# Loads 6 and 7 of a DeltaNet and Fourier-mix kernel: the written order on all engines, and the weight conversion moved within load 6

## The chip, the cores and the metric

The kernel runs on one core of one Trainium2 chip. The metric is the device time of one execution in microseconds (us); the median of three runs of the kernel before is 765.58 us (765.42 to 767.2). The core has a matrix engine (PE, with its weight loads listed as PEld), a vector engine (DVE), an activation engine (ACT), a general engine (POOL) and a queue that issues DMA transfers (SP). Each engine works off a queue of its own.

## The reference

Two stages follow each other. The first is a DeltaNet attention over 4 batches, 8 heads, 768 time steps and a head size of 48; the state is a 48 x 48 matrix per head that each step reads and corrects. The second mixes each batch's 768 x 384 result by the real part of a two-dimensional Fourier transform, normalises each row, and adds a two-layer network of width 1536.

```python
for t in range(S):
    y[:, :, t] = np.einsum('bhd,bhde->bhe', q[:, :, t], state)
    v_old = np.einsum('bhde,bhd->bhe', state, kt)
    state = state + bt[:, :, :, None] * np.einsum('bhd,bhe->bhde', kt, vt - v_old)
...
u = x + np.real(np.fft.fft(np.fft.fft(x, axis=1), axis=2))
un = (u - mu) / np.sqrt(var + 1e-06)
return u + np.maximum(un @ w_ch1, 0.0) @ w_ch2
```

The two weights `w_ch1` (384 x 1536) and `w_ch2` (1536 x 384) arrive as 64-bit floats, and the kernel makes 32-bit floats of them itself from the two halves of each word.

## The kernel before

**Loads and periods.** The time steps are cut into loads of 128, six to a batch, so there are 24 loads, numbered 0 to 23, and load 6 is the first of the second batch. `period(g, side)` (line 1000) writes out the work of one load `g` in six slots (the loop over `i`, line 1049). A slot first takes a step of each generator in `pieces[i]`, then steps of the inversion and of the conversion, then the generators in `behind[i]`, and last some steps of `side`, the network of the batch before.

**The generators.** Each of them issues a few instructions and yields.

- `step(g, c)` (line 678) carries the state over half a load. In the second batch it forms the products `pair<-S,KT`, subtracts them on DVE (`V`, line 698), forms `one<-V,MT`, copies that on ACT (`U`, line 708), forms `pair<-U,K` and adds it to the state on DVE (`S`, line 739, or a copy at line 737 for the first half of a batch).
- `pre_q(g)` (line 531) turns the queries: four PE products, a copy on ACT (line 320), then PE products and a masked product on DVE (`LQ`, line 555).
- `outputs(g)` (line 742) makes the attention's result: PE, a copy on ACT (line 762), PE, an addition on DVE (line 772), and for the first load of a batch one more copy on ACT (line 774).
- `invert16(r)` (line 458) inverts the small triangular matrices of round `r`, four loads to a round. It yields 46 times: a transpose on DVE (line 475, 32 x 32 blocks), a square root on ACT (line 481), eleven short DVE instructions (lines 483 to 504), three at lines 506 to 510, 30 instructions that each need the one before (lines 517 and 520 in turn), and two transposes on DVE (lines 523 and 525). Round 2 is needed by load 8.
- `pre_m16(g)` (line 598) uses that inverse. For load 8 it begins in slot 2 of period 7 with two copies on ACT (`Z`, line 608), and then the PE products `one<-Z,GU`.
- `weight(last)` (line 224) converts one weight in twelve pieces of 128 x 384. A piece `i` is worked in two halves. The first half has an ACT instruction (line 276) and a DVE instruction (line 277) for piece `i` and two ACT instructions (lines 281, 282) for piece `i - 1`. The second half has DVE instructions: line 289 for piece `i - 2`, and lines 293, 297 and 299 for piece `i`. Line 299 frees the staging buffer, and SP then issues the load of piece `i + 3` (line 257). In loads 6 and 7 it is `w_ch2` that is converted; the name `conv` holds this generator.
- `fourier(b)` (line 818) ends in one pass for each 128 rows: PE products, a copy on ACT (`Q`, line 873), four DVE additions (lines 882 to 885), two DVE statistics (lines 889, 890) and two small POOL instructions (lines 893, 894).
- `mlp(b)` (line 898), which is `side`, normalises 256 rows (`un`, two DVE instructions, line 909), turns them (six PE transposes `ptr` and two ACT copies `unT`, line 920), forms the first layer in twelve pieces (`ph`, six matmuls each, with an ACT copy at line 930), and then the second (`po`, line 937, with a DVE addition at line 941).

**The end of the first batch.** Lines 1281 to 1291 write out, one after the other, twelve pieces of `ph`, the conversion's pieces 0 to 7, the last four passes of `fourier(0)`, and at the end `un` for the second group of rows (line 1291). The last pass of `fourier` comes before the conversion's piece 7, and both before this `un`.

**What sets the order.** Inside a `tc.manual_schedule(engines=...)` block, the instructions of the engines that are named stand in their queues in the order in which the code issues them. For other engines the framework's planner orders the queue by its own estimate of when each instruction can go. In the kernel before, the code up to line 1292 and from line 1298 on names PE, DVE, ACT and POOL. Lines 1294 to 1297, which hold the end of `pre_q(6)` and the periods 6 and 7, name PE alone. SP is named nowhere.

In period 6 a slot advances the inversion by 5 and the conversion by 2 (by 4 in the last slot). In period 7 it advances the inversion by 8 in each of slots 0 and 1, which ends it.

Of the kernel before, what the change touches and what calls it, by code (L numbers as in the profile page):

```python
# [64 lines left out]
def kernel(  # L65
# [14 lines left out]
    NL = S // L  # L80
# [56 lines left out]
    def halves(dst, src, g, engine):  # L137
        b, n = divmod(g, NL)
        for c in range(2):
            for hh in range(2):  # L140
                t0 = n * L + c * C
                (engine or nc.sync).dma_start(
                    out=dst[hh * C:hh * C + C, c],
                    in_=src[b, 4 * hh:4 * hh + 4, t0:t0 + C, :].rearrange("j t d -> t j d"))
# [16 lines left out]
    def load_k(g, engine=None):  # L161
        if g < NLT:
            halves(Ks[g % 3].rearrange("p (c j) d -> p c j d", c=2)[:, :, :, 0:D], k, g, engine)

    def load_v(g, engine=None):
        if g < NLT:
            Vs[g] = wk.tile([128, 2, 4, D], F32, tag="V", bufs=2, name="V")
            halves(Vs[g], v, g, engine)
# [3 lines left out]
    def load_beta(r, engine=None):  # L172

        if r * RL >= NLT:
            return
        t = wk.tile([128, W], F32, tag="beta", bufs=2, name="beta")
        i = 0
        while i < RL:
            b, n = divmod(RL * r + i, NL)
            m = min(RL - i, NL - n)  # L180
            for q4 in range(4):
                hh, blk = divmod(q4, 2)
                p0 = q4 * W + i * 8
                src = beta[b, 4 * hh:4 * hh + 4, n * L:(n + m) * L].rearrange(
                    "j (c b t) -> b c j t", b=2, t=W)[blk]
                (engine or nc.sync).dma_start(out=t[p0:p0 + 8 * m], in_=src)
            i += m
        betas[r] = t
# [553 lines left out]
    def outputs(g):  # L742

        b, n = divmod(g, NL)
        pre.pop(g)
        (QT, LQ), U0 = LQs.pop(g), Us.pop(g)
        if n == 0:
            xs[b] = wk.tile([128, NL, DM], F32, tag="x", bufs=2, name="x")
        x = xs[b][:, n, :]
        pq = ps_pair()  # L750
        for j in range(2):
            for hh in range(2):
                for cc in range(2):
                    for jp in range(2):
                        if n == 0 and cc == 0:
                            continue
                        o = (2 * hh + j) * D
                        mm(pq[full[cc], jp, o:o + D], QT[lo[jp], hh, j, cc * C:cc * C + C],
                           S[(b, 2 * n + cc)][lo[jp], hh, j, :], j == 0 and hh == 0)

        rw = full[1] if n == 0 else slice(0, 128)
        nc.scalar.activation(x[rw].rearrange("p (i a e) -> p a i e", a=2, e=D),
                             pq[rw, :, 0:4 * D].rearrange("p a (i e) -> p a i e", e=D), ACT.Copy)
        yield
        pl = ps_pair()
        for j in range(4):
            for cc in range(2):
                for hh in range(2):
                    mm(pl[full[cc], hh, D * j:D * j + D], LQ[full[hh], cc, j, :],
                       U0[full[hh], cc, j, :], j == 0)  # L770
        xv = x.rearrange("p (h e) -> p h e", h=2)
        nc.vector.tensor_tensor(xv[rw], xv[rw], pl[rw, :, 0:4 * D], op=ALU.add)
        if n == 0:
            nc.scalar.activation(xv[full[0]], pl[full[0], :, 0:4 * D], ACT.Copy)
        yield
# [182 lines left out]
    def advance(gen, n=1):  # L958
        for _ in range(n):
            if next(gen, "end") == "end":  # L960
                return False
        return True

    def drain(gen):
        for _ in gen:
            pass
# [33 lines left out]
    def period(g, side):  # L1000


        nonlocal pm, inv, late, done, fold
        b, n = divmod(g, NL)
        r, li = divmod(g, RL)
        more = g + 1 < NLT
        last_round = (r + 1) * RL >= NLT
        load_k(g + 2)
        c0, c1 = step(g, 0), step(g, 1)
        if n > 0:  # L1010
            pieces = [[c0], [c0], [c0], [c1], [c1], [c1]]
        else:
            pieces = [[], [c0], [c0], [c1], [c1], [c1]]
        behind = [[] for _ in range(SLOTS)]
        if late:

            for i in (1, 2) if n == 1 and b == 1 else (0,):
                pieces[i].append(late)
        if n + 1 < NL:
            late = outputs(g)  # L1020
            if g > NL:
                pieces[4].append(late)
        else:

            pieces[5] = []
        fresh = more and li == RL - 1
        if more:
            nq = pre_q(g + 1)
            behind[0].append(nq)
            pieces[2].append(nq)  # L1030
            if g + 1 >= RL * R16:
                pm = pre_m(g + 1)
                pieces[3 if fresh else 1].append(pm)
                pieces[5 if fresh else 3].append(pm)
            elif g + 1 >= 2 * RL:
                pm = pre_m16(g + 1)
                if not fresh:
                    behind[0].append(pm)
                for i in range(4):
                    pieces[i + (2 if fresh else 1)].append(pm)  # L1040
        if not last_round and r > 1:
            if li == 0:
                load_beta(r + 1)
            keys = {0: ((0, 1), (2, 3), (4, 5)), 1: ((0, 1),)}.get(li, ())
            for i, (s0, s1) in enumerate(keys):
                k4 = pre_a(RL * (r + 1) + 3 * li + i)
                behind[s0].append(k4)
                pieces[s1].append(k4)
        for i in range(SLOTS):
            if i == (2 if r + 1 < R16 else 3) and fresh and inv:  # L1050
                drain(inv)
                inv = None
            for p in pieces[i]:
                advance(p)
            if i == 5 and n + 1 == NL:
                o = outputs(g)
                drain(o)
                late = None
            if li == 1 and i == 1 and r > 1 and not last_round:
                inv = invert(r + 1)  # L1060
            if g == NL:
                advance(inv, 5)
                advance(conv, 2 if i < 5 else 4)
            elif inv:
                advance(inv, 8 if r + 1 < R16 else 6)
            if n + 2 >= NL and 0 < i < 5:

                if n + 2 == NL and i == 1:
                    fold = folds(b)
                advance(fold, 2)  # L1070
            at = SLOTS * n + i + 1
            if b > 1:
                want = 2 + (PIECES - KEEP - 2) * at // (SLOTS * NL)
            else:

                want = 2 + KF + (2 + 2 * KF) * at // (2 * SLOTS)
                if n > 1:
                    want = 4 + 3 * KF + (PIECES - KEEP - 4 - 3 * KF) * (at - 2 * SLOTS) // (
                        SLOTS * (NL - 2))
            for p in behind[i]:  # L1080
                advance(p)
            advance(side, want - done)
            done = max(want, done)
        load_v(g + 2)

    engines = {mybir.EngineType.PE, mybir.EngineType.DVE, mybir.EngineType.Activation,
               mybir.EngineType.Pool}
    with tc.manual_schedule(engines=engines):
# [32 lines left out]
        conv = weight(0)  # L1121
# [116 lines left out]
        g = NL - 1  # L1238
# [28 lines left out]
        side, done = mlp(0), 0  # L1267
# [8 lines left out]
        conv = w2s  # L1276
# [14 lines left out]
        advance(side)  # L1291
        done = 3 + KF
        inv = invert16(2)
    with tc.manual_schedule(engines={mybir.EngineType.PE}):
        drain(nq)
        for g in range(NL, NL + 2):
            period(g, side)
    with tc.manual_schedule(engines=engines):
        for b in range(1, B):
            for g in range(max(NL * b, NL + 2), NL * (b + 1)):  # L1300
                period(g, side)

            advance(side, KEEP - 12)
            drain(fold)
            f, then = fourier(b), mlp(b)
            done = 0
            for i in range(4 + NC):
                advance(f)
                advance(side, 12 * (i + 1) // (4 + NC) - done)
                done = 12 * (i + 1) // (4 + NC)  # L1310
                if i in (6, 8):
                    advance(then)
            drain(side)
            side, done = then, 2
        drain(side)
# [30 lines left out]
```

## Time and profile before

| what | value |
|---|---|
| median of three runs | 765.58 us (765.42 to 767.2) |
| the profiled execution, its own time | 767.2 us |
| its span in the profile | 765.3 us |
| mean granted PE clock | 0.955 |
| PE busy | 705.3 us, 92% |
| DVE busy | 378.1 us, 49% |
| ACT busy | 264.3 us, 35% |
| POOL busy | 71.2 us, 9% |

The span runs from the first to the last instruction of the profile; the 1.9 us between the span and the execution's own time lie outside it. All times in the text are counted from the start of the span. The page gives an engine's busy time over the whole span, the views by window give it for a stretch, and the view of waits names for each idle stretch of an engine the instruction that ended it. Busy time of PE can overlap between matmuls, since their ends are modelled.

Periods 6 and 7 lie between about 182 us and 237 us. The stretch from 182 to 192 us has PE busy for 4.18 of 10 us, and DVE for all 10.

### The profile page before, as it was taken

Reading aid. Unit: us, or ns where it says so; the run is one execution under the profiler, and the core shown is the slowest. Engines: PE = TensorE matmul, PEld = TensorE weight load, DVE = VectorE, ACT = ScalarE, POOL = GpSimd, SP = SyncE. Lnnn points to the kernel's source line nnn. Section 1 sums busy time; section 2 is a strip of 40 time slices with the busy share of each in tenths; the row PEclk is TensorE's granted clock in tenths of the full one; section 3 lists DMA queues with packets and bytes.
Section 4 is the critical chain, followed back from the end, with each engine's and each line's share of the span. In section 5 each row is a group of like instructions: output and inputs, shape, how many; then the busy total and the mean of one; then the engine's idle time right before and its main releaser. Section 6 shows DMA issues by size and latency. Waiting matters only on the chain.

```text
span 765.3 us, 23096 instructions
## 1 busy us (share of the span) xinstructions
PE 705.3 (92%) x10198; PEld 542.2 (71%) x10198; DVE 378.1 (49%) x957; ACT 264.3 (35%) x644; POOL 71.2 (9%) x114
## 2 busy tenths in 40 slices
PE   7876788996999987899999999999999999999998
PEld 5676677775866766687867767868677678777684
DVE  5868667479842299625188426369511230700000
ACT  5545554288423422214422333223223222221120
POOL 7000000001000011002110211001100110100000
PEclk8699678998899999999999999999999999999999
DMA  9843332134102321001312221001120000000000
GB/s 152 213 71 80 93 80 54 45 84 134 44 18 65 69 45 39 16 11 32 64 40 44 38 49 39 1 10 43 34 51 16 12 12 1 21 1 21 11 11 21
DMA packets 111862, 36.09 MB, mean 47 GB/s; under 512 B 101873, under 2 KB 109842, under 8 KB 111762
## 3 DMA queue, kind: packets, MB, share of 16 engines
q1 hardware_dynamic: 109938, 33.86, 20.4%
q8 instruction: 80, 1.31, 0.7%
q0 software_dynamic: 640, 0.43, 0.4%
q10 hardware_dynamic: 1184, 0.33, 0.3%
q14 instruction: 20, 0.16, 0.1%
HBM read 29.88 MB, written 4.72 MB: 45 GB/s over the span
## 4 chain that ended last, share of the span: by engine, by line
PE 76%; DVE 15%; ACT 6%; issue 2%; DMA 1%; SPq 0%; ACTq 0%; DVEq 0%
PE po L110 24%; PE ph L110 21%; PE one L110 15%; PE pair L110 10%; PE one L113 2%; PE unread L1101 2%; DVE M L450 1%; DVE tmp L446 1%; PE ptr L113 1%; DVE w L289 1%; DMA C<-in_k_dram 1%; DVE M L520 1%; ACT G L385 1%; DVE tmp L517 1%; PE pf L110 1%
## 5 line engine op out<-in xcount | busy, mean ns | idle before, releaser
L110 PE MATMUL ph<-unT,w 128*128 128x256 f32 x864 | 205.8, 389 | 0.6 <-ACT unT L920 0.6
L110 PE MATMUL po<-w,hT 128*128 128x384 f32 x576 | 205.0, 495 | 0.1
L110 PEld LDWEIGHTS ph<-unT,w 128*128 128x128 f32 x864 | 161.1, 192 | 24.6 <-ACT unT L920 0.9
L110 PEld LDWEIGHTS po<-w,hT 128*128 128x128 f32 x576 | 103.5, 190 | 56.8 <-issue 0.5
L930 ACT ACTIVATE hT<-ph 128x256 f32<-128x256 f32 x144 | 55.3, 384 | 144.8 <-PE ph L110 144.6
L941 DVE TENSOR_TENSOR x<-x,po 128x384 f32<-128x384 f32 x24 | 13.2, 551 | 107.0 <-PE po L110 107.0
L739 DVE TENSOR_TENSOR S<-S,pair 128x192 f32<-128x192 f32 x40 | 14.0, 351 | 76.4 <-PE pair L110 76.3
L110 PEld LDWEIGHTS one<-V,MT 64*64 64x64 f32 x768 | 32.4, 147 | 20.0 <-issue 8.3
L110 PE MATMUL one<-V,MT 64*64 64x48 f32 x768 | 37.7, 234 | 4.2 <-DVE V L698 2.7
L882 DVE TENSOR_TENSOR x<-x,one 128x193 f32<-128x193 f32 x24 | 8.5, 353 | 63.2 <-ACT Q L873 63.2
L450 DVE TENSOR_TENSOR M<-M,tmp 128x31 f32<-128x31 f32 (+15 forms) x93 | 34.7, 373 | 3.2
L446 DVE TENSOR_TENSOR tmp<-A,M 128x31 f32<-128x31 f32 (+15 forms) x93 | 34.1, 367 | 2.5
L110 PE MATMUL one<-MT,ND 64*64 64x64 f32 x768 | 30.6, 234 | 3.5 <-ACT MT L647 3.0
L110 PEld LDWEIGHTS one<-MT,ND 64*64 64x64 f32 x768 | 28.1, 149 | 5.1 <-ACT MT L647 3.4
L698 DVE TENSOR_TENSOR V<-V,pair 128x192 f32<-128x192 f32 x33 | 11.5, 349 | 38.8 <-PE pair L110 30.6
L110 PEld LDWEIGHTS one<-dtab,F 97*128 97x128 f32 (+1 forms) x192 | 25.2, 191 | 5.2 <-ACT F L877 0.5
L110 PEld LDWEIGHTS pair<-U,K 64*64 64x64 f32 x704 | 15.8, 139 | 16.6 <-issue 12.7
L320 ACT ACTIVATE QT<-one 128x512 f32<-128x512 f32 x24 | 14.2, 593 | 38.1 <-PE one L113 38.1
L893 POOL TENSOR_SCALAR rstd<-mv 128x2 f32<-128x2 f32 x12 | 3.9, 325 | 249.4 <-DVE mv L890 249.4
L110 PEld LDWEIGHTS pair<-S,KT 48*64 48x64 f32 x528 | 10.7, 133 | 21.7 <-issue 10.6
L110 PE MATMUL one<-dtab,F 97*128 97x97 f32 (+1 forms) x192 | 25.9, 275 | 0.0
L110 PE MATMUL pair<-KT 48*32 48x64 f32 (+1 forms) x1152 | 21.1, 239 | 4.2 <-ACT KT L320 2.9
(178 smaller groups left out, 1023.8 us busy)
## 6 DMA issues: line engine op xcount, KB each, us to landing
w<-in_moe_w_ch_dram SPq DMA_DIRECT2D x12, 384.0 KB
E<-in_moe_w_ch_dram SPq DMA_DIRECT2D x12, 384.0 KB
out_dram<-x SPq DMA_DIRECT2D x24, 192.0 KB
K<-in_k_dram SPq DMA_DIRECT2D x92, 48.0 KB
V<-in_v_dram SPq DMA_DIRECT2D x92, 48.0 KB
C<-in_k_dram SPq DMA_DIRECT2D x18, 192.0 KB
Q<-in_q_dram SPq DMA_DIRECT2D x18, 192.0 KB
w<-in_q_dram SPq DMA_DIRECT2D x6, 192.0 KB
```

Of the source, the lines that this page charges most:

```text
L110: nc.tensor.matmul(o, lhsT=lhsT, rhs=rhs, start=start, stop=stop, skip_group_check=True)
L113: nc.tensor.matmul(o, lhsT=src, rhs=ident[0:src.shape[0], 0:src.shape[0]], is_transpose=True, start=start, stop=True, skip_group_check=True)
L289: nc.vector.tensor_tensor(dst, man0.rearrange("p (c f) -> p c f", c=c), num0.bitcast(F32).rearrange("p (c f) -> p c f", c=c), op=ALU.mult)
L320: nc.scalar.activation(dst.rearrange("p h j t -> p (h j t)"), pt, ACT.Copy)
L446: nc.vector.tensor_tensor(t, A[:, j + 1:W, j:j + 1].broadcast_to([128, n, j + 1]), M[:, j:j + 1, 0:j + 1].broadcast_to([128, n, j + 1]), o ...
L450: nc.vector.tensor_tensor(M[:, j + 1:W, 0:j + 1], M[:, j + 1:W, 0:j + 1], t, op=ALU.add)
L698: nc.vector.tensor_tensor(R4, R4, pw[:, :, 0:2 * D].rearrange("p a (j e) -> p a j e", e=D), op=ALU.subtract)
L739: nc.vector.tensor_tensor(s1v, s0.rearrange("p h j e -> p h (j e)"), pk, op=ALU.add)
L882: nc.vector.tensor_tensor(near, near, pb[:, 0, 0:MH + 1], op=ALU.add)
L930: nc.scalar.activation(hT[:, fc, :], ph, ACT.Relu)
L941: nc.vector.tensor_tensor(x[:, T, :], x[:, T, :], po, op=ALU.add)
L1101: nc.tensor.matmul(unread[:, 0:DM], lhsT=src[:, 0:128], rhs=src, start=True, stop=True, skip_group_check=True)
```

## The change

The change has two parts. The periods 6 and 7, and the end of `pre_q(6)`, move into the block that names PE, DVE, ACT and POOL. In period 6, the slot's five steps of the inversion are split: three stay where they were, and two come at the slot's end, after the conversion's steps, which move there too, behind `behind[i]` and `side`.

```diff
             if g == NL:
-                advance(inv, 5)
-                advance(conv, 2 if i < 5 else 4)
+                advance(inv, 3)
             elif inv:
                 advance(inv, 8 if r + 1 < R16 else 6)
...
             advance(side, want - done)
             done = max(want, done)
+            if g == NL:
+                advance(conv, 2 if i < 5 else 4)
+                advance(inv, 2)
         load_v(g + 2)
...
         inv = invert16(2)
-    with tc.manual_schedule(engines={mybir.EngineType.PE}):
         drain(nq)
-        for g in range(NL, NL + 2):
-            period(g, side)
-    with tc.manual_schedule(engines=engines):
         for b in range(1, B):
-            for g in range(max(NL * b, NL + 2), NL * (b + 1)):
+            for g in range(NL * b, NL * (b + 1)):
                 period(g, side)
```

`NL` is 6. No instruction is added or taken out; PE's order is the same as before, since PE is named in both.

## The prediction

> **What bounds the kernel now.** I read the page first: PE is busy 92% of the span, and in the windows from 195 to 262 us nearly always, so a delay there moves the end by as much. The exception near the change is the window 182 to 192 us. There I asked for PE's waits (the numbers are us in total, times, longest):
>
> ```profile
> PE ptr L113 <- DVE un L909: 5.8, 1, 5.8
> ...
> PE one L110 <- DVE V L698: 0.9, 1, 0.9
> ```
>
> These two are the stalls that the change can touch: 5.8 us before the transposes of `un`, and 0.9 us in period 7. The timeline shows the first one (start, duration, engine, line):
>
> ```profile
> 181.91 1.99 DVE L475 STREAM_TRANSPOSE A<-G 128x1024 f32<-128x1024 f32 x1 [0.33 <-ACT G L385]
> ...
> 182.94 0.35 ACT L873 ACTIVATE Q<-one 128x193 f32<-128x193 f32 x1
> ...
> 183.82 0.32 DVE L882 TENSOR_TENSOR x<-x,one 128x193 f32<-128x193 f32 x1
> ...
> 184.36 0.29 ACT L481 ACTIVATE nrm<-A 128x32 f32<-128x32 f32 x1
> ...
> 188.68 0.86 DVE L909 TENSOR_SCALAR un<-x,mv,rstd 128x384 f32<-128x384 f32 x2
> ...
> 189.30 1.51 PE L113 MATMUL ptr<-pack,un 128*128 128x128 f32 x6 [5.82 <-DVE un L909]
> ```
>
> The planner has put the inversion's transpose (L475), written after `un`, ahead of the last Fourier pass (L882), while DVE had nothing else to do. It also put L481 ahead of ACT's other work. The written order takes both back. PE's clock falls with the idle stretch (columns: length, PE, PEld, DVE, ACT, POOL busy, granted clock, DMA):
>
> ```profile
> 120.74:124.15 3.41, 1.26 (x72) 1.01 (x68) 2.30 (x7) 2.17 (x4) 0.00 (x0) 1.00 0.25 48
> 182.18:185.59 3.41, 1.30 (x37) 0.98 (x36) 3.41 (x7) 3.41 (x11) 0.00 (x0) 1.00 0.61 167
> 185.59:189.01 3.42, 0.00 (x0) 0.00 (x0) 3.42 (x11) 1.38 (x4) 2.19 (x2) 0.50 0.03 6
> 189.01:192.42 3.41, 3.12 (x24) 2.64 (x25) 3.41 (x14) 2.54 (x6) 0.18 (x1) 0.50 0.37 115
> 192.42:195.83 3.41, 3.41 (x10) 2.69 (x9) 2.89 (x10) 2.31 (x6) 0.00 (x0) 0.50 0.33 115
> ```
>
> The granted clock changes only on the edges of such 3.41 us windows. [...] So `ph` x12 took 4.85 us here against 2.86 us later.
>
> **Part 1, the opening of period 6.** In the written order DVE, free at 181.58, waits for ACT's `Q` copy (182.94 + 0.35 = 183.29). Then come the pass's additions (start to start 0.26 each) and statistics, done at 185.2; conversion piece 7 (0.25 + 0.47 + 0.5 + 0.55 + 0.26, about 2.0 us); `un` starts at 187.2 and the transposes of `un` at 187.7. That is 1.6 us earlier than 189.30, since L475, L555 and another piece's L289 no longer stand in between.
>
> The gain does not get through. `un` is followed on DVE by L555 of load 6 (0.6 us) and then by L475 (2.0 us), to 190.6. On ACT the written order is L481, the copy of the turned queries (L320, 0.59 us), the two copies `unT` (L920, 0.49 us each). L481 needs L475, so all of them queue behind it: 190.6 + 0.28 + 0.5 + 0.4 + 0.5 gives `unT` at 192.2. PE has `one<-V,MT` in between (to 190.6 at half clock) and then waits 1.6 us. `ph` starts at 192.2 against 191.77. **Term: +0.4 us**, of which 0.3 is left at `pair<-U,K` (the clock returns at 195.83 in both).
>
> **Part 2, the slots of period 6.** A slot has two `ph` pieces, 2.78 us. The conversion's ACT step (L276) now queues behind the slot's two `ph` copies, and DVE's L293 behind L276. The second `ph` of slot 1 ends at about 196.9; its copy and L276 take to 197.8; L293, L297, L299 and two inversion steps take to 199.5. Then slot 2 stands on DVE in sequence: L737, L555, three inversion steps (1.6 us), the conversion (2.2 us), L506 to L517 (0.9 us): L698 starts at about 204.0 and ends at 204.4. PE is done with slot 3's `ph` at 203.7 and waits for it 0.7 us. In the trace of before L698 ran at 201.65, ahead of that work, and hid behind `ph`. From slot 4 on there is slack: L739 ends at 209.5 and period 7's first product comes at 212.35 (211.21 before). **Terms 1 and 2 together: +1.1 us.**
>
> **Part 3, period 7.** The timeline of before:
>
> ```profile
> 211.21 0.45 PE L110 MATMUL pair<-S,KT 48*64 48x48 f32 x16
> ...
> 213.59 1.92 DVE L525 STREAM_TRANSPOSE A<-M 128x1024 f32<-128x1024 f32 x1
> ...
> 215.35 0.34 DVE L698 TENSOR_TENSOR V<-V,pair 128x192 f32<-128x192 f32 x1
> ...
> 220.65 0.56 DVE L772 TENSOR_TENSOR x<-x,pair 64x384 f32<-64x384 f32 x1 [0.16 <-PE pair L110]
> 221.06 1.11 PE L110 MATMUL one<-Z,GU 64*64 64x64 f32 x32
> 221.24 0.48 ACT L774 ACTIVATE x<-pair 64x384 f32<-64x384 f32 x1 [3.22 <-DVE x L772]
> ```
>
> From the first product to `one<-Z,GU` PE takes 9.85 us, 0.92 of it the wait for L698 behind L525. The written order puts L698 ahead, which gives the 0.92 us back: 8.9 us. But there the copies `Z` (L608) stand on ACT behind L774, which needs L772, which stands on DVE behind L698, the last 14 inversion steps, both transposes and L739. In sum, from the first product's start: 0.5 (product) + 0.3 + 4.0 (14 steps at about 0.25 and 0.04 between dependent ones) + 2.0 + 1.85 + 0.3 + 0.55 + 0.5 (L774) + 0.9 (two L608) = 10.9 us. PE waits 0.65 us for L739 and 1.1 us for `Z`. **Term: 10.9 - 9.85 = +1.0 us.** After it the order is the same, with DVE idle enough.
>
> **What else moves.** The twelve pieces' DVE and ACT work is the same in number. The last two loads of staged weights follow L299: 187.3 and 194.1 instead of 188.8 and 191.8; a piece landed some 3.6 us after its issue (181.64, ACT released at 185.24) and piece 11 is read at about 203.6, so 5 us cover it. If that cover were gone, DVE would wait for it. SP's next loads wait for PE anyway (197.04). On POOL the zeroing of `M` (L474, 1.0 us, at 75.7 before) moves to period 6 and the scaling of V (L629, 0.83 us) to the end of period 7; POOL is idle there. A DVE step took 0.77 us beside L629 where its neighbours took 0.24, so each may cost DVE 0.5 us or nothing; nothing is my value, since the rows L893 and L894 (1.2 us) beside DVE work stretched themselves and not DVE. A gain there is excluded, as nobody waited for them.
>
> **The sum.** 1.1 + 1.0 = +2.1 to 2.2 us against the profiled execution's own 767.2 us: 769.4 us. The median is 1.6 us lower. I take that as one half-clock window less (3.41 us at half speed is 1.7 us): with the window edges 0.3 us later, 189.01:192.42 would have been full. In the written order the wait of 1.6 us before `ph` keeps that window from being full, so I measure from 767.2. Against the median this is +3.8 us. If the two waits of part 3 (1.75 us) fall into one window, PE is busy 1.66 us of it, at the edge of half, and another window at half clock adds 1.7 us: 771.1.
>
> [...]
>
> **Rivals.**
> - The clock falls in period 7 too: 771.1, and up to 772.7 with 0.5 us each from POOL's two moves and 0.6 us more in the slots.
> - No change: 765.6. DVE's work is the same in sum and is spread; if the slots lose nothing (L698 early enough by 0.7 us), and period 7's chain comes out 1 us shorter, the opening's 0.4 us is left and the clock returns a window early. For it speaks that each margin is under 1.2 us.
> - Faster: `un` comes 1.6 us earlier and `unT` follows it directly. Place: ACT's queue at 188 to 192 us; it decides if L475 is done before the transposes of `un` end (about 189.2). Then `ph` starts at 190.6, 1.1 us early, part 3 gives 0.9 us, and the clock is as in the median: 765.6 - 2.0 = 763.6, or 762 with a further window saved. Against it: L475 comes after `un` and L555 in the code.
> - The change does nothing, if the planner's order was the written one: 765.6. The timeline excludes this (L475 before L882).
>
> **How the numbers follow.** Forecast 769.4: 0.40; clock falls again, 771 to 772.7: 0.30; no change: 0.17; faster: 0.13. About 0.3% (2.3 us) is what a measurement can tell from no change, so "same" is 763.3 to 767.9. The first two cases are slower: 0.70; same 0.17; faster 0.13. The range leaves out the faster case and the far end above: 765.3 to 772.7.
>
> **What would show it.** Part 1: the transposes of `un` near 187.7, ACT's L920 directly after L320 and L481, PE waiting for `unT`. Part 2: PE's second `one<-V,MT` waiting for L698. Part 3: `one<-Z,GU` waiting for L608, and L608 after L774. I am wrong if L920 runs before L481, or if L698 of slot 3 ends before slot 3's `ph`.

## The result and the profile after

The changed kernel takes 770.35 us (median of 4 runs, 769.85 to 770.54) against 765.5 us before: a ratio of 1.0059, 95% interval 1.0042 to 1.0077. It is slower by 0.6%, as forecast, and the time lies within the range, 0.95 us above the predicted 769.4. The profiled execution has a span of 768.6 us, 3.3 us more than before.

PE's order is the same in both kernels, so the n-th matmul of one trace can be set against the n-th of the other. Up to the changed stage the after profile runs 2.7 us ahead, with 51.2 us at half clock before 180 us where the other has 54.6. This has nothing to do with the change, which only begins there. To leave it out I compare a **stretch**: from the start of `pair<-QT,KT` of load 6 to the start of `one<-Z,ND` in period 7. Before:

```profile
182.20 0.69 PE L110 MATMUL pair<-QT,KT 48*64 48x64 f32 x32
...
228.66 1.11 PE L110 MATMUL one<-Z,ND 64*64 64x64 f32 x32
```

After:

```profile
179.54 0.69 PE L110 MATMUL pair<-QT,KT 48*64 48x64 f32 x32
...
229.79 1.11 PE L110 MATMUL one<-Z,ND 64*64 64x64 f32 x32
```

That is 46.46 us before and 50.25 us after: the stretch grew by 3.8 us. The span's 3.3 us are these 3.8, less the 2.7 ahead of the stretch, and 2.2 more behind it (most of them while 10.2 us at half clock stand between 240 and 330 us, where before it was 3.4). Of the 4.85 us between the medians the stretch of these two profiles holds 3.8; where the rest lies is not shown.

Where the stretch grew, the waits of PE show (window 175 to 260 us, those inside the stretch; us in total, times, longest):

```profile
PE ptr L113 <- DVE un L909: 4.8, 1, 4.8
PE ph L110 <- ACT unT L920: 1.7, 1, 1.7
PE one L110 <- ACT Z L608: 1.3, 1, 1.3
PE one L110 <- DVE V L698: 0.7, 1, 0.7
PE pair L110 <- DVE S L739: 0.6, 1, 0.6
```

Two waits of before became five. The first is shorter (4.8 for 5.8), the 0.9 us for V L698 in period 7 is gone, and four new ones, 4.3 us in sum, took their place. In sum PE waits 2.4 us longer (9.1 for 6.7). The timeline of the opening after the change:

```profile
180.27 0.35 ACT L873 ACTIVATE Q<-one 128x193 f32<-128x193 f32 x1
...
180.65 0.36 DVE L882 TENSOR_TENSOR x<-x,one 128x193 f32<-128x193 f32 x1 [1.73 <-ACT Q L873]
...
184.31 0.73 DVE L299 TENSOR_SCALAR O<-E 128x384 int32<-128x384 int32 x1
184.96 0.85 DVE L909 TENSOR_SCALAR un<-x,mv,rstd 128x384 f32<-128x384 f32 x2
...
186.33 1.91 DVE L475 STREAM_TRANSPOSE A<-G 128x1024 f32<-128x1024 f32 x1
...
188.28 0.26 ACT L481 ACTIVATE nrm<-A 128x32 f32<-128x32 f32 x1 [5.80 <-DVE A L475]
...
188.92 0.86 ACT L920 ACTIVATE unT<-ptr 128x384 f32<-128x384 f32 x2
...
189.84 4.51 PE L110 MATMUL ph<-unT,w 128*128 128x256 f32 x12 [1.73 <-ACT unT L920]
```

DVE now stands idle for 1.73 us where the planner had put L475. ACT stands idle for 5.80 us in front of L481, with the copies `unT` behind it. In period 7, first the copies `Z` of the kernel before, then the kernel after:

```profile
213.74 0.91 ACT L608 ACTIVATE Z<-G,pack 128x256 f32<-128x256 f32 x2 [2.04 <-DVE G L523]
```

```profile
210.26 0.35 DVE L698 TENSOR_TENSOR V<-V,pair 128x192 f32<-128x192 f32 x1 [1.33 <-PE pair L110]
...
216.51 1.92 DVE L525 STREAM_TRANSPOSE A<-M 128x1024 f32<-128x1024 f32 x1
...
218.64 0.56 DVE L772 TENSOR_TENSOR x<-x,pair 64x384 f32<-64x384 f32 x1
...
219.62 0.90 ACT L608 ACTIVATE Z<-G,pack 128x256 f32<-128x256 f32 x2
...
220.66 1.98 PE L110 MATMUL one<-Z,GU 64*64 64x64 f32 x32 [1.30 <-ACT Z L608]
```

L698 is ahead of the transposes now, and `Z`, copied at 213.74 before (2.5 us after the period's first product), comes 9.9 us after that product (209.74). The clock, by windows (length, PE, PEld, DVE, ACT, POOL busy, granted clock, DMA):

```profile
217.12:220.53 3.41, 1.62 (x81) 1.35 (x80) 2.74 (x4) 1.28 (x3) 0.00 (x0) 1.00 0.16 29
220.53:223.95 3.42, 3.29 (x34) 2.65 (x35) 0.00 (x0) 1.28 (x3) 0.00 (x0) 0.50 0.02 5
```

The two waits of period 7 left PE busy for 1.62 us of a window, and the next window ran at half clock: `one<-Z,GU` took 1.98 us instead of 1.11. The longer waits (2.4 us) and this window (1.4 us, by the run with unread products in period 7 below) make up the 3.8 us.

### The profile page after: what moved, and what is told of

The parts are those of the page before. It is cut to its first block, busy times and chain, and to the rows that moved or that the text cites. A ratio compares the mean times of both kernels' runs of the same rounds, so it can differ in the third digit from the quotient of the medians.

```text
span 768.6 us, 23101 instructions
## 1 busy us (share of the span) xinstructions
PE 708.8 (92%) x10198; PEld 544.6 (71%) x10198; DVE 380.9 (50%) x957; ACT 263.8 (34%) x644; POOL 69.5 (9%) x114
## 4 chain that ended last, share of the span: by engine, by line
PE 74%; DVE 15%; ACT 7%; issue 2%; DMA 1%; SPq 0%; ACTq 0%; DVEq 0%
PE po L110 23%; PE ph L110 22%; PE one L110 15%; PE pair L110 9%; PE one L113 2%; PE unread L1103 2%; DVE M L450 1%; DVE tmp L446 1%; PE ptr L113 1%; DMA C<-in_k_dram 1%; ACT GU L395 1%; ACT G L385 1%; PE pf L110 1%; DVE LQ L555 1%; DVE w L289 1%
## 5 line engine op out<-in xcount | busy, mean ns | idle before, releaser
L110 PE MATMUL ph<-unT,w 128*128 128x256 f32 x864 | 207.9, 392 | 2.4 <-ACT unT L920 2.4
L739 DVE TENSOR_TENSOR S<-S,pair 128x192 f32<-128x192 f32 x40 | 14.0, 351 | 71.2 <-PE pair L110 71.2
L698 DVE TENSOR_TENSOR V<-V,pair 128x192 f32<-128x192 f32 x33 | 11.5, 350 | 42.0 <-PE pair L110 38.6
L110 PEld LDWEIGHTS pair<-S,KT 48*64 48x64 f32 x528 | 10.7, 133 | 20.1 <-issue 10.9
```

What stands on the lines that cost most here:

```text
L110: nc.tensor.matmul(o, lhsT=lhsT, rhs=rhs, start=start, stop=stop, skip_group_check=True)
L698: nc.vector.tensor_tensor(R4, R4, pw[:, :, 0:2 * D].rearrange("p a (j e) -> p a j e", e=D), op=ALU.subtract)
L739: nc.vector.tensor_tensor(s1v, s0.rearrange("p h j e -> p h (j e)"), pk, op=ALU.add)
```

## The experiments

The times are medians; beside each experiment the kernel before was run on that experiment's chip (765.89 to 765.95 us; the two first rows are from the first comparison). The last column is the stretch in the profile, in which differences outside of the changed stage don't show.

| kernel | us | ratio, 95% interval | stretch, us |
|---|---|---|---|
| before | 765.5 | | 46.46 |
| after | 770.35 | 1.0059 (1.0042 to 1.0077) | 50.25 |
| written order alone | 769.82 | 1.0057 (1.0044 to 1.0070) | 50.55 |
| slots' split alone | 765.78 | 0.9997 (0.9986 to 1.0008) | 46.40 |
| after, L475 and L481 ahead | 766.02 | 1.0000 (0.9990 to 1.0011) | 45.86 |
| after, Z ahead of L774 | 766.44 | 1.0004 (0.9994 to 1.0015) | 47.23 |
| after, 2 unread products in period 7 | 768.62 | 1.0036 (1.0023 to 1.0049) | 48.84 |
| after, 6 unread products in the opening | 768.57 | 1.0037 (1.0024 to 1.0051) | 50.27 |
| after, conversion behind L698 | 769.88 | 1.0054 (1.0037 to 1.0072) | 50.31 |
| after, L475, L481 and Z ahead | 765.48 | 0.9993 (0.9983 to 1.0002) | 44.37 |
| the same, 6 unread products | 763.70 | 0.9962 (0.9947 to 0.9976) | 43.05 |
| before, 6 unread products in the opening | 762.67 | 0.9958 (0.9945 to 0.9971) | 42.92 |

**The two parts of the change, each alone.** First the written order with the slots as before (against the changed kernel):

```diff
             if g == NL:
-                advance(inv, 3)
+                advance(inv, 5)
+                advance(conv, 2 if i < 5 else 4)
...
-            if g == NL:
-                advance(conv, 2 if i < 5 else 4)
-                advance(inv, 2)
```

> Periods 6 and 7 in the written order on all engines, but with the slots as before (five inversion steps and the conversion ahead of the queries' turn and the network). My theory (the loss comes from the written order: unT behind the inversion's square root on ACT, Z behind L774 and L772): unT comes later still, since the conversion's ACT steps also stand ahead of it; laid out by rows the Fourier-mix network's first ph of period 6 starts 1.6 us later than in the changed kernel and one<-Z,GU 1.8 us later, so 771 to 773 us. Rival (the loss comes from moving the conversion to the slot's end): as before, 764.5 to 767 us.

It took 769.82 us, below the expected 771 to 773. The queue did what was expected: the first `ph` starts 11.87 us after the stretch's start instead of 10.30 (1.6 us later), `one<-Z,GU` 42.92 instead of 41.12 (1.8 us later). What was missing is the half clock of period 7: the same waits of 0.6 and 1.3 us lay over two windows, with PE busy for 82% and 62%, and the clock did not fall. PE did not wait for L698 in slot 3. The rival, 764.5 to 767, is out.

The second part alone is the kernel before with the slot's lines of the change, and the planner still ordering DVE, ACT and POOL (the lines of the diff without those that move the periods).

> The inversion's split and the conversion at the slot's end, with the planner still ordering DVE, ACT and POOL in periods 6 and 7. My theory: the planner fills DVE and ACT again and L475 stands ahead of L882, so near the kernel before, 764 to 767 us. Rival (the move of the conversion costs by itself): 769 to 771 us.

765.78 us, ratio 0.9997: no difference. Its timeline shows that the planner undid the written place again:

```profile
181.32 1.98 DVE L475 STREAM_TRANSPOSE A<-G 128x1024 f32<-128x1024 f32 x1 [0.33 <-ACT G L385]
...
183.20 0.34 DVE L882 TENSOR_TENSOR x<-x,one 128x193 f32<-128x193 f32 x1
```

So the loss belongs to the written order, and the split's own share is small: it brings `unT` 1.6 us earlier than the order alone.

**The opening.** In the changed kernel the inversion begins earlier:

```diff
         for fc in range(KF):
...
+            if fc == 10:
+                inv = invert16(2)
+                advance(inv)
             if fc % 3 == 1:
                 advance(f)
...
+        advance(inv)
         advance(side)
         done = 3 + KF
-        inv = invert16(2)
...
             if g == NL:
-                advance(inv, 3)
+                advance(inv, 3 if i else 1)
```

> The changed kernel, with the inversion's transpose L475 written ahead of the last Fourier pass and its square root L481 ahead of un. My theory: L475 falls into DVE's wait for Q, un keeps its time within 0.5 us, unT no longer waits, ph starts 1.6 us earlier, V L698 of slot 3 2.5 us earlier so that PE no longer waits for it; one<-Z,GU 2.5 us earlier, and perhaps one half-clock window less (1.7 us): 766 to 768 us. Rival (the opening is no matter, the slots and period 7 carry the loss): 769.5 to 770.5 us.

766.02 us. The transpose fell into DVE's wait, and `unT` follows the transposes of `un` at once:

```profile
180.24 1.99 DVE L475 STREAM_TRANSPOSE A<-G 128x1024 f32<-128x1024 f32 x1 [0.33 <-ACT G L385]
...
186.65 1.42 PE L113 MATMUL ptr<-pack,un 128*128 128x128 f32 x6 [4.85 <-DVE un L909]
187.47 1.13 ACT L920 ACTIVATE unT<-ptr 128x384 f32<-128x384 f32 x2 [3.37 <-PE ptr L113]
188.00 1.09 PE L110 MATMUL one<-V,MT 64*64 64x48 f32 x16
189.03 3.41 PE L110 MATMUL ph<-unT,w 128*128 128x256 f32 x12
```

`ph` starts 8.51 us after the stretch's start (10.30 in the changed kernel): 1.8 us earlier, 1.6 expected. The half clock lasted one window here instead of three. One point was wrong: PE still waited 0.73 us for L698 in slot 3, as PE had come earlier by as much as DVE. One edit of order takes back the whole loss, against the rival. Part of that came by the clock of period 7. The two waits there (0.6 and 1.3 us) are still in the profile, but they lie over two windows, with PE busy for 81% and 63%, and the clock held. By the run with unread products in period 7 below, this is about 1.4 of the 4.4 us by which the stretch is shorter than in the changed kernel.

**Period 7.** The copies `Z` are written at the end of slot 1:

```diff
-        if g != 2 * RL:
-            yield
+        yield
...
                 advance(inv, 8 if r + 1 < R16 else 6)
+                if g == NL + 1 and i == 1:
+                    advance(pm)
```

> The changed kernel, with the two copies Z (L608) of load 8 written at the end of period 7's slot 1, ahead of L774 on ACT; PE's order is the same. My theory: Z is ready before PE comes, the wait of 1.3 us before one<-Z,GU goes and with it the half-clock window behind it (1.5 us): 767.5 to 769.2 us, and one<-Z,GU starts right after pair<-QT,KT. Rival (PE waits for something else there, L739 or a buffer): 770 to 770.6 us.

766.44 us, and the stretch is 3.0 us shorter than after. `one<-Z,GU` follows `pair<-QT,KT` without a wait and takes 1.11 us again:

```profile
220.77 0.69 PE L110 MATMUL pair<-QT,KT 48*64 48x64 f32 x32 [0.62 <-DVE S L738]
...
221.28 1.11 PE L110 MATMUL one<-Z,GU 64*64 64x64 f32 x32
```

(The lines are one lower in this kernel.) The time is 1.1 us below the expected 767.5 to 769.2. The stretch fell by 3.0 us where 1.3 for the wait and 1.5 for the clock were expected; in the profile more was gained outside of it, where 6.8 us at half clock stand between 240 and 330 us instead of 10.2. That this set the median is not shown.

**The clock.** In the wait before `one<-Z,GU`, and in the opening's wait, products that nobody reads (`spin(n)` issues `n` of them on PE; they only keep it busy):

```diff
             for p in pieces[i]:
+                if g == NL + 1 and i == 2 and p is pm:
+                    spin(2)
                 advance(p)
```

> The changed kernel with two unread PE products (2 x 0.68 us, nothing reads them) put into PE's wait of 1.3 us before one<-Z,GU in period 7. My theory (the two waits there, 0.6 and 1.3 us, make a window with PE busy under half, and the clock halves behind it): Z is no earlier, one<-Z,GU starts at the same time within 0.1 us, and the half-clock window behind it is gone, 1.5 us less: 768.5 to 769.3 us. [...]

768.62 us, within the theory's 768.5 to 769.3. The half-clock window of period 7 is gone and the stretch is 1.4 us shorter, though PE had the two products (1.56 us) more to do.

```diff
             for p in behind[i]:
                 advance(p)
+            if g == NL and i == 0:
+                spin(6)
```

This edit was made in the kernel before and in the changed kernel.

> The kernel before (planner's order) with the same six unread products in the opening's wait. My theory of the opening (its price is the idle 5.8 us and the half clock after it): the idle stays, the half clock goes; but DVE is full up to L525 in that order and V L698 of period 7 waits behind it, so of the 3 us at most 2 come through: 763.3 to 764.7 us. Rival (the half clock is hidden behind DVE): 765.5 to 766 us.

> The changed kernel with the same six unread products in the opening's wait for un that took 3.3 us off the kernel before. My theory (in the changed kernel unT is held by L475 and L481 in DVE's and ACT's queues, not by PE): ptr and one<-V,MT take 1 us less, but PE then waits that much longer for unT (about 3 us instead of 1.7), ph starts at the same time, and little is gained: 768.5 to 770.5 us. Rival (the half clock of the opening is what the opening costs, as in the kernel before): 766.8 to 767.8 us.

In the kernel before it gave 762.67 us, a little below the expected 763.3 to 764.7, the stretch 3.5 us shorter where at most 2 were expected to come through. At `pair<-U,K` of period 6 PE is 2.9 us ahead of the kernel before, which is the opening. The other 0.7 us comes in period 7, where the planner's order came out differently: L698 stands ahead of L525 (211.22 and 211.45), and PE waits 0.25 us for it instead of 0.92. In the changed kernel the stretch did not move at all (50.27 for 50.25):

```profile
180.66 4.04 PE L1105 MATMUL unread<-evt 128*128 128x384 f32 x12
...
185.55 0.91 PE L113 MATMUL ptr<-pack,un 128*128 128x128 f32 x6 [0.86 <-DVE un L909]
...
189.79 4.54 PE L110 MATMUL ph<-unT,w 128*128 128x256 f32 x12 [2.74 <-ACT unT L920]
```

`ptr` took 0.91 us instead of 1.51, and PE's wait for `unT` grew from 1.73 to 2.74 us; `ph` starts 10.26 us after the stretch's start (10.30). This tells the two openings apart best: before, PE's own pace set the opening; after, the queues of DVE and ACT do. The kernel's median is 1.8 us below that of the changed kernel all the same. The profile puts that outside of the stretch (3.4 us at half clock between 240 and 330 us, for 10.2); the two ratios' intervals overlap, so I don't count it as a gain.

**The slots.** In the changed kernel, slot 2's conversion moves behind L698:

```diff
-                advance(conv, 2 if i < 5 else 4)
+                advance(conv, {2: 0, 3: 4, 5: 4}.get(i, 2))
```

> The changed kernel with slot 2's conversion steps of period 6 moved behind V L698 in slot 3. My first term for the slots says that L698 queues 0.7 us too late behind them; laid out by rows, L698 then comes 1.9 us earlier and PE's wait for it goes, but the ACT copy U (L708) now queues behind two pieces of the conversion in slot 4 and gives the 0.7 us back: 769.9 to 770.5 us, the wait named V L698 gone and one for U L708 in its place. Rival (the wait goes and nothing takes its place): 769 to 769.8 us.

769.88 us, and the stretch is the same as after (50.31). The wait for L698 is gone and another has come:

```profile
PE pair L110 <- ACT U L708: 0.5, 1, 0.5
```

PE's wait for L739 in period 7 also grew, from 0.6 to 1.0 us. The median lies between the two ranges, 0.02 us below the theory's and 0.08 above the rival's; the waits decide for the theory.

**Both ends, and a faster version.** The edits of the opening and of period 7 together, without and with the six unread products of the opening:

> The changed kernel with both edits of the runs before: L475 and L481 written ahead of the last Fourier pass and of un, and the copies Z ahead of L774. My theory (the two waits are separate, one in the opening and one in period 7): the second edit still takes 1.3 us off the first one's 766.0: 764 to 765 us. Rival (one wait only moves when the other goes, so that the gains are the same one): 765.7 to 766.5 us.

765.48 us, in neither range. The stretch fell by 1.5 us more than with the opening's edit alone (44.37 for 45.86), so the two waits are separate; 0.5 us of it is left in the median, whose intervals overlap. The profile has 10.2 us at half clock between 240 and 330 us, the other 6.8. That this took the gain back is read from one profile of each, not shown for all runs.

> As the run with both edits, and six unread PE products (4.07 us) in PE's wait for un at the opening of period 6. My theory: PE waits no less for un, but the clock stays at full speed there, ptr, one<-V,MT and the first ph take 2 us less, and the rest of the period follows, as DVE has time: 762 to 763.5 us, faster than before. Rival (DVE sets the pace of period 6, so PE's faster clock is lost waiting for L698): 764 to 765 us.

763.70 us, 0.2 above the range of the theory and below the rival's. The stretch fell to 43.05. It is no better than the kernel before with the same unread products: 762.67 us, ratio 0.9958 (0.9945 to 0.9971), the fastest here. The written order, with its two faults mended, brings nothing over the planner's that the medians show; PE's wait for L698 in slot 3 (0.9 us here) is left in it.

## Why the prediction was right

**Part 1, the opening.** Right in its mechanism. The transposes of `un` started 1.1 us earlier than before by the stretch, not 1.6: the additions and statistics came 0.1 later, and L299 beside POOL's zeroing of `M` took 0.73 us instead of 0.35, the cost from POOL that I had set at nothing with a bound of 0.5. (It took 0.72 to 0.73 us in all six kernels in which the zeroing stands there, and 0.38 at most in the six others.) `ph` was 0.7 us late (predicted 0.4), and 0.4 was left at `pair<-U,K` (0.3). The runs with L475 ahead and with unread products show that the queue behind L481 holds `unT`.

**Part 2, the slots.** PE waited 0.73 us for L698 (predicted 0.7), and period 7's first product came 1.19 us late (1.1). But as the run with the conversion moved showed, this wait is a place where DVE's and ACT's load shows, more than a cause of its own.

**Part 3, period 7.** The way from the first product to `one<-Z,GU` took 10.92 us (predicted 10.9), with waits of 0.61 and 1.30 us (0.65 and 1.1). It is the term that was met best.

**The clock in period 7.** The forecast case left it at full speed, with the fall as a second case (771.1). In the profile after, it fell, and the stretch grew by 3.8 us against 3.9 for that case (2.2 and 1.7). In the profiles of five kernels with both waits it fell in three and stayed in two: in the three PE was busy for 41 to 47% of one window, in the two the waits lay over two windows, each at least 62% busy. The unread products in period 7 show the price: 1.4 us of the stretch.

**The baseline, and luck.** I measured from 767.2 and not from the median, taking the 1.6 us between them for a half-clock window of the opening that the other executions did not have. No run shows this, nor that PE has to be busy for the whole of a window before the clock comes back: in the profile after it came back after windows with 3.39 us (189.81:193.23) and 3.29 us (220.53:223.95). The two profiles in the planner's order without added products, the kernel before and the split alone (766.6 us), both have three such windows in the opening (10.2 us), as the profile after has. What sets the profile before apart lies ahead of the change: 54.6 us at half clock before 180 us, the most of the twelve profiles (44.4 to 54.6), and the latest start of the stretch, 182.20 us (179.53 to 182.11 in the others). So the sum held 1.6 us that no run bears out, and it left out the fall of the clock in period 7, 1.7 us in the second case, which came. That case set an edge at half of a window, which no run shows (the last section has the windows), and in the run with unread products the fall's price was 1.4 us. The 1.6 and the 1.7 us nearly cancel: from the median, the second case gives 765.5 + 3.9 = 769.4 as well. The waits were foreseen; that the time came within 1 us is in part luck.

**Short waits and the clock.** In the profile after, the waits of 0.61 and 1.30 us left PE busy for 1.62 us of a window, and the clock halved; filling the second one with two products (1.56 us) kept it. In the profile before, the clock halved after the window 120.74:124.15 with PE busy for 1.26 us, where PE's longest wait was 1.65 us, for `U` of L720. In neither window did PE wait longer than 1.65 us at a time.

**The rival on the faster side.** Its condition was L475 done before the transposes of `un` end. The run with L475 ahead made that true, and `ph` came 1.1 us earlier than before by the stretch (8.51 for 9.57), as the rival had it. It gave 766.0 us and not 763.6. The waits of slot 3 (0.7 us) and of period 7 (0.6 and 1.3 us) stood in its profile, and the rival had left them out. With `Z` ahead as well, the stretch is 2.1 us shorter than before (44.37 for 46.46), about the rival's 2.0, but the median shows only 0.5 us of it (765.48 for 765.95).

## What to carry to other kernels

Before an order is written out over several engines, follow each queue by itself: in the changed kernel ACT stood idle for 5.80 us in front of a 0.26 us square root that waited for DVE, with the copies `unT` written behind it, and PE waited 1.7 us for these. Look for the long instruction that the planner had put into an idle stretch, and write it there too. Where PE must wait, see whether PE's pace sets what follows before adding products that nobody reads: six of them made the stretch 3.5 us shorter in the kernel before, and in the changed kernel it stayed (50.27 us for 50.25).

## What was not expected of the hardware

Against what I read from the profile before, PE's busy time in a window did not tell by itself whether the granted clock changed after it. The windows are the stretches of 3.41 us that the records of the clock give: in the profiles before and after, all its changes (16 and 18) lie whole multiples of 3.41 us apart. In the profile before, the clock halved after seven windows with PE busy for 1.26 to 1.66 us (37 to 49%) and after the window 8.10:11.51 with 2.09 us (61%), but not after 298.23:301.65 with 1.88 us (55%). In the profile with both ends mended a window with PE busy for 1.52 us (45%) kept the clock:

```profile
293.08:296.49 3.41, 1.52 (x11) 1.04 (x7) 3.20 (x10) 0.45 (x2) 0.00 (x0) 1.00 0.39 101
296.49:299.90 3.41, 3.41 (x75) 2.87 (x75) 3.20 (x10) 0.98 (x2) 0.62 (x1) 1.00 0.25 51
```

In the profile after, the clock doubled after the window 220.53:223.95 with 3.29 us (96%), where it had stayed at half after the 3.12 us (91%) of 189.01:192.42 before the change, and it stayed at half after a window with all 3.41 us (312.69:316.10). Busy time of PE is modelled in these profiles, which may be a part of it. What sets the half-clock windows between 240 and 330 us, 3.4 to 10.2 us of them in these twelve profiles, was not followed.
